# Attention, a dense layer and a routed mixture of experts on one core: who makes the low parts of the first weights, and how chunk 0 opens

## The chip, the cores and the metric

The kernel runs on one core of one Trainium2 chip. The metric is the device time of one execution in microseconds (us). Three runs of the kernel before gave 1522.58, 1522.92 and 1523.56 us, median 1522.92 us.

The engines by the names of the profile: PE (TensorE; PEld are its weight loads), DVE (VectorE), ACT (ScalarE), POOL (GpSimd) and SP (SyncE, which here only issues DMAs). Matrix products land in PSUM, in eight banks of 128 partitions by 512 float32 columns; everything else on the chip is SBUF.

## What is computed

```python
kv = np.einsum('bhsd,bhse->bhde', k, v)
out = np.einsum('bhsd,bhde->bhse', q, kv)
rms = np.sqrt(np.mean(out * out, axis=-1, keepdims=True) + 1e-06)
x = out / rms * g_norm                    # then heads side by side: 4608 tokens x 512
h = np.maximum(np.maximum(x @ w1, x @ w2), x @ w3)
x = h @ w_out                             # 512 -> 768 -> 512
logits = x @ w_gate + np.log1p(np.exp(x @ w_noise)) * noise
top2 = np.argpartition(-logits, 2, axis=1)[:, :2]
...
h = np.maximum(x[mask] @ w1[e], 0.0)      # 8 experts, 512 -> 1024 -> 512
out[mask] += top2_w[mask, k, None] * (h @ w2[e])
```

There are 8 batches of 576 tokens and 8 heads of 64.

## The kernel before

**Precision.** A float32 product is made of three faster ones. Each operand is split into a high part, which ACT rounds, and a low part, which is the operand less its high part; the passes are high x high, high x low and low x high (`g1_mm`: 12 matmuls of 512 or 256 columns for one group of 128 features).

**Tokens.** The 4608 tokens go in nine chunks of 512. A chunk is attended (`ao`, 64x64 products of Q with K-transposed-V), normalized, transposed (`xtrans_pe`) and split (`xtrans_hi` on ACT, `xtrans_lo` on DVE). The dense layer then takes 18 groups (`g1`), three for each 128 of the 768 hidden features, of which `g1_top` keeps the maximum in `HM` (the first of three by ACT, the others by DVE, both out of PSUM); `hsplit` splits it and `g2` multiplies by w_out. `route_a` and `route_b` pick the experts on DVE, and `scatter` writes rows to DRAM by indirect DMAs on POOL. Eight batches of 576 do not match nine chunks of 512, so chunk 1's first 256 tokens are done early, inside chunk 0 (the groups `eq`, which read the tiles `xA`, B_87 below).

**Chunk 0 and its weights.** The twelve weight slabs of the dense layer, W0 to W11 (W_70 to W_81 below; nine for w1 to w3, three for w_out), arrive as raw 64-bit halves and are made in chunk 0, one after another: `conv_lo` (ACT), `conv_hi` (two DVE instructions, lines 509 and 510), `conv_sq` (ACT), `conv_add` (DVE, line 518), `conv_top` (DVE, line 531), `conv_split` (ACT, line 535, the high part) and `conv_rest` (DVE, line 539, the low part). `conv_rest` reads two SBUF tiles and writes a third. A slab feeds two groups.

**The order in chunk 0** is set by a small planner (`task` and `run_tasks`): each task has an engine, a cost in us, the tasks it comes after, and an urgency; `run_tasks` appends the tasks to the engines' queues in the order in which they could start by these costs. At run time each engine takes its queue strictly in that order and waits where an input isn't there.

**K and V.** `kv_mm` makes K-transposed times V of a pair of heads from 576 rows: four steps of 128 rows and a last one of 64. For the last step the 64 rows stand in tiles whose other 64 partitions POOL has filled with zeros, so that all five steps have the same shape. For batch 0 the steps are the outer loop and the four pairs the inner one, each pair in a bank of its own; for the other batches `kv_pair` does a pair at a time, all four in one bank, which `kv_out` copies at once.

**The experts.** After chunk 8 the tokens are taken in units of 512, 256 or 128 rows of one expert (`unit`; `G1` and `G2` are its two products). The routing of chunk 8 and the table of units (`table`, a generator) run on DVE within the first units: `pump` says how many pieces of it go into which step. One step is one call of `G1` and what is due from `G2`.

```python
pump = {0: 1, 2: 1, 3: 2, 4: 2, 5: 2, 6: 2, 8: 1, 9: 1}
...
for _ in range(pump.get(step[0], 0)):
    next(tg, None)
```

Of the kernel before, what the change touches and what calls it, by code (L numbers as in the profile page):

```python
# [88 lines left out]
def body(tc, A, dbg=None):  # L89
# [61 lines left out]
    kvraw = {}  # L151

    def quarters(t):
        return [t[:, i * 512:(i + 1) * 512] for i in range(4)]

    def load_kv(b, part):
        if part == 0:
            SP.dma_start(KV0, A["kv4"][b, 0])
            kvraw[b] = [quarters(KV0)]
        elif part == 1:  # L160
            t = STG[b % 2]
            SP.dma_start(t, A["kv4"][b, 1])
            kvraw[b].append(quarters(t))
        else:
            t = STG[2]
            SP.dma_start(t[0:64, 0:1024], A["kvr"][b])
            kvraw[b].append((t[:, 0:512], t[:, 512:1024]))

    qbuf = [RB, KV0] + [RB] * 7

# [4 lines left out]
        SP.dma_start(qbuf[c][:, 0:2048], A["qT"][c])  # L175

    pad = st("pad", [128, XW])
    POOL.memset(HM[0][64:128, :], 0.0)
    POOL.memset(pad[64:128, 0:512], 0.0)
    POOL.memset(ones, 1.0)  # L180
    POOL.memset(RA[:, 2048:], 0.0)

# [2 lines left out]

    def kv_mm(b, p, s, out):
        r = kvraw[b]
        if s < 4:
            k, v = r[s // 2][2 * (s % 2):2 * (s % 2) + 2]
        else:  # L190
            k, v = r[2]
        for h in range(2):
            o = p * 128 + h * 64
            PE.matmul(out[HALF[h], :], k[:, o:o + 64], v[:, o:o + 64], start=s == 0, stop=s == 4)  # L194

    def kv_pair(b, p, bank):
        for s in range(5):
            kv_mm(b, p, s, bank[:, p * 64:(p + 1) * 64])

    def kv_out(b, bank):  # L200
        DVE.tensor_copy(KB[b % 2], bank[:, 0:256])

    ao_bank = {}

# [373 lines left out]
    load_w1(1)  # L578
    for f in (conv_lo, conv_hi, conv_sq, conv_add, conv_top, conv_split, conv_rest):
        f(0)  # L580
    for p in range(4):
        abank()
    for s in range(5):
# [5 lines left out]
    for p in range(4):  # L589
        (ACT.copy if p % 2 else DVE.tensor_copy)(KB[0][:, p * 64:(p + 1) * 64], AC[p][:, 0:64])  # L590

    zeroed = []

# [55 lines left out]
    def on_ring(name, n=1):  # L649
        return (name, n)  # L650
# [6 lines left out]
    for i in range(4):  # L657
        task(f"n0c{i}", "DVE", 0.65, ["n0b2"], lambda i=i: norm_c(0, i), 0)

        def t0(i=i):  # L660
            tr0[i] = xtrans_pe(0, i, None if i < 3 else abank())

        task(f"t0{i}", "PE", 0.44, [f"n0c{i | 1}"] + ([f"t0{i - 1}"] if i else []), t0, 0,
             on_ring(f"x0l{i}") if i < 3 else None)
# [3 lines left out]
    def kv1(p):  # L668
        if p == 0:
            bank_of["kv"] = hbank()  # L670
        kv_pair(1, p, bank_of["kv"])

    for p in range(4):
        task(f"kvp{p}", "PE", 0.6, ["kv1"] + [f"kvp{p - 1}" if p else "first0"], lambda p=p: kv1(p), 1,
             None if p else on_ring("kvo"))
    task("kvo", "DVE", 0.42, ["kvp3", "hi0"], lambda: kv_out(1, bank_of["kv"]), 0.3)
    task("q1", "SP", 2.6, ["kvp3", "w1"], lambda: load_q(1), 0)
    task("tri", "SP", 0.2, ["kvp3", "q1"], lambda: SP.dma_start(pad[:, 0:128], A["cst"][:, CST["tri"][0]:]), 9)

    for s in range(1, 12):  # L680
        if s > 1:
            task(f"w{s}", "SP", 2.6, [["kv1", "top0"], ["kvp3"], ["top1"]][s - 2] + [f"w{s - 1}"] if s < 5 else [f"top{s - 3}", f"w{s - 1}"], lambda s=s: load_w1(s), s)
        free_t = [f"add{s - 2}"] if s > 1 else []
        free_w = [f"rest{s - 2}"] if s > 1 else []
        if s == 11:
            free_w = free_w + ["gate_a0"]
        u = 2 + 0.1 * s if s > 1 else 0.4
        task(f"lo{s}", "ACT", 1.15, [f"w{s}"] + ["n0e"] * (s == 1), lambda s=s: conv_lo(s), u)
        task(f"op{s}", "DVE", 1.92, [f"w{s}"] + free_t + ["n0c3"] * (s == 1), lambda s=s: conv_hi(s), u)
        task(f"sq{s}", "ACT", 1.14, [f"op{s}"], lambda s=s: conv_sq(s), u - 1 if s > 1 else 0.05)  # L690
        task(f"add{s}", "DVE", 1.22, [f"op{s}", f"lo{s}"], lambda s=s: conv_add(s), u)
        task(f"top{s}", "DVE", 1.22, [f"add{s}", f"sq{s}"] + free_w, lambda s=s: conv_top(s), u)
        task(f"hi{s}", "ACT", 1.06, [f"top{s}"], lambda s=s: conv_split(s), u - 1)
        task(f"rest{s}", "DVE", 1.22, [f"hi{s}"], lambda s=s: conv_rest(s), u - 1)

    def passes(g, z):
        if g not in bank_of:
            bank_of[g] = abank() if g < 2 else hbank()
        for n in z:
            g1_mm(g, bank_of[g], n)  # L700
# [261 lines left out]
    for c in range(NCH):  # L962
        if c == NCH - 1:
            ctx1.close()
            sb2 = ctx.enter_context(tc.tile_pool(name="sb2", bufs=1, reuse_waits="tile"))
            xTu.append(xview(B2, sb2.tile([128, 2048], FR, name="xlo")))
        for g in range(18):
            misc1(c, g)
            if c > 0:
                g1(c, g)  # L970
        if c == 0:
            run_tasks({"PE": 16.8, "DVE": 19.0, "ACT": 18.2, "SP": 13.5},
                      {f"{n}0": (12.0, "DVE") for n in ("w", "lo", "op", "sq", "add", "top", "hi", "rest")})
        window(c)

# [300 lines left out]
def layout(q, k, v, g_norm, moe_w1, moe_w2, moe_w3, moe_w_out,  # L1276
# [34 lines left out]
```

## Time and profile before

| | |
|---|---|
| median of three runs | 1522.92 us (1522.58 to 1523.56) |
| the profiled execution, its own time | 1517.31 us |
| its span, first to last instruction | 1515.5 us |
| PE busy | 1489.0 us, 98% |
| PE's weight loads | 1279.2 us, 84% |
| DVE busy | 777.5 us, 51% |
| ACT busy | 658.6 us, 43% |
| POOL busy | 224.0 us, 15% |
| share of PE in the chain that ended last | 96% |

The profile comes from one execution; its time stands beside its span in the table, and the difference lies outside the span. Busy shares are of the span. The ends of matmuls are modelled, so that two neighbours can seem to overlap by some tenths of a us; a start-to-start distance is the safer reading. Chunk 0 fills the span up to about 118 us, chunks 1 to 8 the part up to about 680 us, and the experts the rest.

### The profile page before, as it was taken

The numbers are of one execution on the slowest core, as the hardware profiler recorded it, in microseconds if no ns is written. First come the engines' busy times: TensorE is split into PE (matmuls) and PEld (weight loads), VectorE is DVE, ScalarE is ACT, GpSimd is POOL, SyncE is SP. The second block draws the span as 40 slices with busy tenths as digits, with TensorE's granted clock in tenths as the row PEclk, the third lists the DMA queues.
The fourth block names the chain that finished last, engine by engine and source line by source line (L and its number), as shares of the span: only waits on it lengthen the run. The fifth ranks groups of instructions, "written<-read, shape, count | busy, mean of one in ns | idle before, by whom it ended". The sixth has DMA issues, their size and how long they took to land.

```text
span 1515.5 us, 23040 instructions
## 1 busy us (share of the span) xinstructions
PE 1489.0 (98%) x9268; PEld 1279.2 (84%) x9268; DVE 777.5 (51%) x1503; ACT 658.6 (43%) x1024; POOL 224.0 (15%) x331
## 2 busy tenths in 40 slices
PE   6999999999999999999999999999999999999997
PEld 5889989898989888898888888888888888888886
DVE  6985535454444445458444463544554544635443
ACT  4553424242424233343444454644654544536443
POOL 0000211112020202014111101201211111012012
PEclk9999999999999999999999999999999999999999
DMA  8322434142332303082777566745876665668444
GB/s 314 134 77 91 138 132 153 72 147 85 126 117 95 120 29 120 8 251 113 228 169 155 143 199 163 203 133 131 212 187 153 184 148 142 205 167 209 128 116 79
DMA packets 160340, 218.74 MB, mean 144 GB/s; under 512 B 125472, under 2 KB 125728, under 8 KB 143712
## 3 DMA queue, kind: packets, MB, share of 16 engines
q1 hardware_dynamic: 140272, 165.45, 35.3%
q0 software_dynamic: 19952, 51.73, 15.1%
q8 instruction: 74, 1.21, 0.3%
q14 instruction: 42, 0.34, 0.1%
HBM read 137.91 MB, written 51.72 MB: 125 GB/s over the span
## 4 chain that ended last, share of the span: by engine, by line
PE 96%; DVE 1%; DMA 1%; ACT 1%; issue 0%; POOL 0%; SPq 0%; POOLq 0%; DVEq 0%
PE bank L356 29%; PE bank L1185 27%; PE bank L1123 26%; PE bank L402 10%; PE bank L216 1%; PE bank L194 1%; PE bank L1137 1%; DMA RB<-qT 1%; PE bank L554 0%; DVE stat L237 0%; PE bank L546 0%; POOL out L1159 0%; PE bank L1148 0%; PE bank L275 0%; ACT B L279 0%
## 5 line engine op out<-in xcount | busy, mean ns | idle before, releaser
L356 PE MATMUL bank<-B,W 128*128 128x512 f32 (+1 forms) x2160 | 452.7, 369 | 2.3 <-DVE B L284 1.4
L356 PEld LDWEIGHTS bank<-B,W 128*128 128x128 f32 x2160 | 375.0, 188 | 70.6 <-ACT B L279 1.6
L1185 PE MATMUL bank<-W,B 128*128 128x512 f32 x1728 | 417.8, 390 | 0.0
L1185 PEld LDWEIGHTS bank<-W,B 128*128 128x128 f32 x1728 | 322.2, 188 | 65.3
L1123 PE MATMUL bank<-B,W 128*128 128x512 f32 (+1 forms) x1568 | 364.2, 370 | 0.0
L1123 PEld LDWEIGHTS bank<-B,W 128*128 128x128 f32 x1568 | 280.6, 188 | 52.4
L338 DVE TENSOR_TENSOR W<-G,W 128x1024 fp32r<-128x1024 f32 x184 | 222.6, 1224 | 116.5 <-ACT W L337 115.9
L1127 ACT ACTIVATE B<-bank 128x512 fp32r<-128x512 f32 (+1 forms) x160 | 88.7, 555 | 349.4 <-PE bank L1123 349.3
L1128 DVE SCALAR_TENSOR_TENSOR B<-bank,B 128x512 fp32r<-128x512 f32 (+1 forms) x160 | 101.9, 637 | 258.5 <-ACT B L1127 258.0
L337 ACT ACTIVATE W<-G 128x1024 fp32r<-128x1024 f32 x184 | 192.0, 1055 | 40.4 <-PE bank L1185 27.3
L402 PE MATMUL bank<-W,B 128*128 128x256 f32 (+1 forms) x1296 | 160.9, 284 | 0.3 <-DVE B L364 0.3
L402 PEld LDWEIGHTS bank<-W,B 128*128 128x128 f32 x1296 | 159.5, 188 | 1.4 <-DVE B L364 0.5
L475 POOL DMA_INDIRECT Xg<-RA,si x72 | 71.0, 986 | 516.6 <-issue 362.6
L374 DVE TENSOR_TENSOR hm<-hm,bank 128x512 f32<-128x512 f32 (+1 forms) x106 | 69.5, 656 | 115.0 <-PE bank L356 109.8
L360 ACT ACTIVATE B<-hm 128x512 fp32r<-128x512 f32 (+1 forms) x53 | 32.1, 606 | 183.1 <-DVE hm L374 183.1
L1159 POOL DMA_INDIRECT out<-xn,idt x37 | 60.5, 1635 | 264.4 <-ACT xn L1190 257.1
L1123 PE MATMUL bank<-xlo,W 128*128 128x512 f32 (+1 forms) x352 | 83.8, 360 | 0.0
L1123 PEld LDWEIGHTS bank<-xlo,W 128*128 128x128 f32 x352 | 61.3, 189 | 10.0
L1159 POOL DMA_INDIRECT out<-hm,idt x19 | 31.0, 1630 | 222.4 <-ACT hm L1190 219.4
L1159 POOL DMA_INDIRECT out<-x2T,idt x19 | 31.4, 1652 | 177.2 <-ACT x2T L1190 173.7
L372 ACT ACTIVATE hm<-bank 128x512 f32<-128x512 f32 (+1 forms) x53 | 30.3, 572 | 59.8 <-PE bank L356 49.2
L409 ACT COPY RA<-bank 128x256 uint16<-128x256 uint16 x72 | 25.7, 373 | 68.2 <-DVE RA L409 62.7
(196 smaller groups left out, 1047.9 us busy)
## 6 DMA issues: line engine op xcount, KB each, us to landing
G<-mw SPq DMA_DIRECT2D x92, 1024.0 KB, 5.0
G<-w1s SPq DMA_DIRECT2D x12, 1024.0 KB, 4.8
kv<-kv SPq DMA_DIRECT2D x8, 1024.0 KB, 7.2
G<-kv SPq DMA_DIRECT2D x8, 1024.0 KB, 10.7
RB<-qT SPq DMA_DIRECT2D x8, 1024.0 KB, 4.9
out<-pad POOLq DMA_DIRECT2D x5, 1280.0 KB, 5.7
out<-pad POOLq DMA_DIRECT2D x2, 1536.0 KB, 6.4
G<-kvr SPq DMA_DIRECT2D x6, 256.0 KB, 10.6
```

Of the source, the lines that this page charges most:

```text
L337: ACT.activation(w[:, 0:1024], src, AF.Copy)
L338: DVE.tensor_tensor(w[:, 1024:2048], src, w[:, 0:1024].bitcast(F), op=OP.subtract)
L356: PE.matmul(bank[:, 0:t1 - t0], w_in(g)[:, a, k, s], x[b][:, k, t0:t1], start=n == 0 and k == 0, stop=n == 2 and k == 3)
L360: ACT.activation(hTf(f)[:, 0, t0:t1], hm, AF.Copy)
L374: DVE.tensor_tensor(hm, hm, bank, op=OP.max)
L402: PE.matmul(x2b[i][z][:, 0:hi - lo], h[:, a, s], w[:, b, lo:hi], start=f == 0 and n == 0, stop=f == 5 and n == 2)
L475: i = POOL.indirect_dma_start(out=Xg, out_offset=bass.IndirectOffsetOnAxis(ap=idx, axis=0), in_=src, in_offset=None)
L1123: PE.matmul(bank[:, 0:n], w[:, a, k, s], x[b][:, k, 0:n], start=z == 0, stop=z == 11)
L1127: ACT.activation(h[:, 0, 0:n], bank[:, 0:n], AF.Relu)
L1128: DVE.scalar_tensor_tensor(h[:, 1, 0:n], bank[:, 0:n], 0.0, h[:, 0, 0:n].bitcast(F), op0=OP.max, op1=OP.subtract)
L1159: d = POOL.indirect_dma_start(out=A["out"], out_offset=bass.IndirectOffsetOnAxis(ap=idt[u % 3][:, i:i + 1], axis=0), in_=y, in_offset=None ...
L1185: PE.matmul(obank[i], h[:, a, s], w[:, b, ff % 2, :], start=ff == 0 and n == 0, stop=ff == 7 and n == 2)
```

## The change

Four things are changed. **(a)** The low part of each slab but the first is made by POOL, with the same instruction, and the planner gets a clock for POOL. **(b)** Chunk 0's first two groups are done in two halves of 256 tokens, each half with its three passes as soon as its tokens are split, in four banks instead of two; the fourth transpose takes a bank of the other ring. **(c)** The last 64 rows of K and V lie by heads, the pairs 0 and 1 in the lower 64 partitions and the pairs 2 and 3 in the upper; their products have 64 rows and no zeros; a batch's pairs come one after another, each with its four full steps in a bank of its own, then the last steps of the pairs in the order 0, 2, 1, 3; the copies out of the four banks are shared by DVE and ACT. POOL's three fills with zeros are gone, and one DMA takes the place of two. **(d)** The first pieces of the table go into other steps of the experts' first unit. The numbers of lines after line 178 shift: line 539 becomes 542, 356 becomes 359, 194 becomes 193, 374 becomes 377.

```diff
-            SP.dma_start(t[0:64, 0:1024], A["kvr"][b])
-            kvraw[b].append((t[:, 0:512], t[:, 512:1024]))
+            SP.dma_start(t[:, 0:512], A["kvr"][b])
+            kvraw[b].append(t[:, 0:512])
...
-    POOL.memset(HM[0][64:128, :], 0.0)
-    POOL.memset(pad[64:128, 0:512], 0.0)
...
-        if s < 4:
-            k, v = r[s // 2][2 * (s % 2):2 * (s % 2) + 2]
-        else:
-            k, v = r[2]
         for h in range(2):
-            o = p * 128 + h * 64
+            if s < 4:
+                k, v = r[s // 2][2 * (s % 2):2 * (s % 2) + 2]
+                o = p * 128 + h * 64
+            else:
+                k, v = r[2][HALF[p // 2], 0:256], r[2][HALF[p // 2], 256:512]
+                o = p % 2 * 128 + h * 64
             PE.matmul(out[HALF[h], :], k[:, o:o + 64], v[:, o:o + 64], start=s == 0, stop=s == 4)
...
+    def kv_all(b, banks):
+        for p in range(4):
+            for s in range(4):
+                kv_mm(b, p, s, banks[p][:, 0:64])
+        for p in (0, 2, 1, 3):
+            kv_mm(b, p, 4, banks[p][:, 0:64])
+
+    def kv_outs(b, banks):
+        for p in range(4):
+            (ACT.copy if p % 2 else DVE.tensor_copy)(KB[b % 2][:, p * 64:(p + 1) * 64], banks[p][:, 0:64])
...
-        DVE.tensor_tensor(lo, t, hi.bitcast(F), op=OP.subtract)
+        (POOL if s else DVE).tensor_tensor(lo, t, hi.bitcast(F), op=OP.subtract)
...
-    for s in range(5):
-        for p in range(4):
-            kv_mm(0, p, s, AC[p][:, 0:64])
+    first = [abank() for p in range(4)]
+    kv_all(0, first)
...
-            tr0[i] = xtrans_pe(0, i, None if i < 3 else abank())
+            tr0[i] = xtrans_pe(0, i)
...
+    task("kvp3", "PE", 2.3, ["kv1", "first100"], kv1, 1, on_ring("kvo", 4))
...
-        task(f"rest{s}", "DVE", 1.22, [f"hi{s}"], lambda s=s: conv_rest(s), u - 1)
+        task(f"rest{s}", "POOL", 2.3, [f"hi{s}"], lambda s=s: conv_rest(s), u - 1)
+
+    def half_pass(g, x, n):
+        if not half_of:
+            half_of.update({(a, b): abank() for a in range(2) for b in range(2)})
+        g1_mm(g, half_of[g, x], n, xT, x * 256, x * 256 + 256)
+
+    def half_top(g):
+        for x in range(2):
+            g1_top(g, half_of[g, x][:, 0:256], HM[0][:, x * 256:x * 256 + 256])
...
-    for z in range(3):
-        task(f"first{z}", "PE", 1.82, [["x0h3", "hi0", "n0c2"], ["x0l3", "first0"], ["rest0", "first1"]][z],
-             lambda z=z: (passes(0, [z]), passes(1, [z])), 2)
+    for g in range(2):
+        for x in range(2):
+            for z in range(3):
+                task(f"first{g}{x}{z}", "PE", 0.48,
+                     [[f"x0h{2 * x + 1}", "hi0"], [f"x0l{2 * x + 1}"], ["rest0"]][z] + [f"first{g}{x}{z - 1}"] * (z > 0),
+                     lambda g=g, x=x, z=z: half_pass(g, x, z), 2 + 0.1 * g)
...
-            POOL.memset(STG[2][64:128, 0:1024], 0.0)
...
-            bank = abank()
-            for p in range(4):
-                kv_pair(c + 1, p, bank)
-            kv_out(c + 1, bank)
+            banks = [abank() for p in range(4)]
+            kv_all(c + 1, banks)
+            kv_outs(c + 1, banks)
...
-            run_tasks({"PE": 16.8, "DVE": 19.0, "ACT": 18.2, "SP": 13.5},
+            run_tasks({"PE": 16.8, "DVE": 19.0, "ACT": 18.2, "SP": 13.5, "POOL": 10.0},
...
-    pump = {0: 1, 2: 1, 3: 2, 4: 2, 5: 2, 6: 2, 8: 1, 9: 1}
+    pump = {0: 1, 3: 2, 4: 2, 5: 2, 6: 3, 8: 1, 9: 1}
...
-    a["kvr"] = kv[:, 512:].reshape(NB, 64, 1024)
+    a["kvr"] = kv[:, 512:].reshape(NB, 64, 2, 2, 256).transpose(0, 3, 1, 2, 4).reshape(NB, 128, 512)
```

What this does to the engines' queues, at three places. **PE, batch 0's K and V**, the first products of the program (kv_92 holds the first two steps' rows, G_84 the next two's, hm_96 the last 64; bank_109 to bank_112 are the pairs' banks). Before, rows 5 to 12 of the queue, which follow four that are the same as the first four here:

```order
L194 MATMUL bank_109<-kv_92 64x64 x2
L194 MATMUL bank_110<-kv_92 64x64 x2
L194 MATMUL bank_111<-kv_92 64x64 x2
L194 MATMUL bank_112<-kv_92 64x64 x2
L194 MATMUL bank_109<-G_84 64x64 x2
L194 MATMUL bank_110<-G_84 64x64 x2
L194 MATMUL bank_111<-G_84 64x64 x2
L194 MATMUL bank_112<-G_84 64x64 x2
```

Now, rows 1 to 12:

```order
L193 MATMUL bank_109<-kv_92 64x64 x4
L193 MATMUL bank_109<-G_84 64x64 x4
L193 MATMUL bank_110<-kv_92 64x64 x4
L193 MATMUL bank_110<-G_84 64x64 x4
L193 MATMUL bank_111<-kv_92 64x64 x4
L193 MATMUL bank_111<-G_84 64x64 x4
L193 MATMUL bank_112<-kv_92 64x64 x4
L193 MATMUL bank_112<-G_84 64x64 x4
L193 MATMUL bank_109<-hm_96 64x64 x2
L193 MATMUL bank_111<-hm_96 64x64 x2
L193 MATMUL bank_110<-hm_96 64x64 x2
L193 MATMUL bank_112<-hm_96 64x64 x2
```

All sixteen products with kv_92 stood ahead of the first that needs G_84; now four of them do.

**PE, the groups of the weight slabs 3 to 5** (W_73 to W_75; a row of 512 columns that reads B_85 is chunk 0's, a row of 256 that reads B_87 is one of chunk 1's early groups, whose weights are older). Before:

```order
L356 MATMUL bank_106<-B_85,W_73 128x512 x8
L356 MATMUL bank_107<-B_87,W_71 128x256 x12
L356 MATMUL bank_106<-B_85,W_73 128x512 x4
L356 MATMUL bank_108<-B_85,W_73 128x512 x12
L356 MATMUL bank_105<-B_85,W_74 128x512 x8
L356 MATMUL bank_106<-B_87,W_72 128x256 x12
L356 MATMUL bank_105<-B_85,W_74 128x512 x4
L356 MATMUL bank_107<-B_85,W_74 128x512 x12
L356 MATMUL bank_108<-B_85,W_75 128x512 x8
L356 MATMUL bank_105<-B_87,W_72 128x256 x12
L356 MATMUL bank_108<-B_85,W_75 128x512 x4
L356 MATMUL bank_106<-B_85,W_75 128x512 x12
```

Now, up to slab 6:

```order
L359 MATMUL bank_107<-B_85,W_73 128x512 x8
L359 MATMUL bank_108<-B_87,W_70 128x256 x12
L359 MATMUL bank_107<-B_85,W_73 128x512 x4
L359 MATMUL bank_105<-B_85,W_73 128x512 x12
L359 MATMUL bank_106<-B_87,W_70 128x256 x12
L359 MATMUL bank_107<-B_85,W_74 128x512 x12
L359 MATMUL bank_108<-B_85,W_74 128x512 x12
L359 MATMUL bank_105<-B_85,W_75 128x512 x12
L359 MATMUL bank_106<-B_85,W_75 128x512 x12
L359 MATMUL bank_107<-B_85,W_76 128x512 x12
L359 MATMUL bank_108<-B_85,W_76 128x512 x12
L359 MATMUL bank_105<-B_87,W_71 128x256 x12
```

From slab 3's first row to slab 8's last there were six early groups in PE's queue, and there are three now; ahead of slab 3 there were three and there are none. The other fifteen stand between and behind the transposes of the last three slabs (line 549, `gate_a`).

**DVE, two slabs in the middle of chunk 0.** Before:

```order
L539 TENSOR_TENSOR W_73<-RA,W_73 128x1024
L518 ISA G_83<-G_83,RB 128x1024x2
L531 SCALAR_TENSOR_TENSOR RA<-G_83 128x1024
L509 TENSOR_SCALAR RB<-G_82 128x1024
L510 SCALAR_TENSOR_TENSOR RB<-G_82,RB 128x1024
L374 TENSOR_TENSOR hm_96<-hm_96,bank_108 128x512
L539 TENSOR_TENSOR W_74<-RA,W_74 128x1024
L518 ISA G_82<-G_82,RB 128x1024x2
L374 TENSOR_TENSOR xn_93<-xn_93,bank_106 128x256
L531 SCALAR_TENSOR_TENSOR RA<-G_82 128x1024
```

Now:

```order
L521 ISA G_83<-G_83,RB 128x1024x2
L534 SCALAR_TENSOR_TENSOR RA<-G_83 128x1024
L512 TENSOR_SCALAR RB<-G_82 128x1024
L513 SCALAR_TENSOR_TENSOR RB<-G_82,RB 128x1024
L377 TENSOR_TENSOR hm_96<-hm_96,bank_105 128x512
L377 TENSOR_TENSOR xn_93<-xn_93,bank_106 128x256
L521 ISA G_82<-G_82,RB 128x1024x2
L534 SCALAR_TENSOR_TENSOR RA<-G_82 128x1024
```

The low parts (line 539) are gone from DVE; eleven rows of line 542 stand in POOL's queue, one behind another, ahead of what POOL does for chunk 0's routing.

## Rows read from the trace of the kernel before

**Rows 1.** Busy time by stretches: us, then each engine's busy us, granted clock, DMA share, GB/s.

```profile
49.20:95.00 45.80, 45.79 (x249) 39.62 (x250) 43.23 (x50) 25.24 (x29) 0.00 (x0) 1.00 0.41 139
```

**Rows 2.** PE's waits: line, what for, us in total, times, longest.

```profile
PE bank L356 <- DVE B L284: 1.4, 1, 1.4
...
PE bank L356 <- ACT B L279: 0.9, 1, 0.9
PE bank L460 <- DVE Cb L448: 0.8, 1, 0.8
...
PE bank L546 <- DVE RA L531: 0.5, 1, 0.5
```

**Rows 3.** Timeline, 8 to 18 us: start, us, what [idle before <-releaser].

```profile
8.11 1.98 PE L194 MATMUL bank<-kv 128*64 128x64 f32 x32 [8.11 <-DMA kv<-kv]
...
11.02 1.97 PE L194 MATMUL bank<-G 128*64 128x64 f32 x32 [0.93 <-DMA G<-kv]
...
12.78 1.07 PE L194 MATMUL bank<-pad,hm 128*64 128x64 f32 x16
...
14.53 3.11 PE L216 MATMUL bank<-kvt,RB 64*64 64x64 f32 x128 [0.68 <-DMA RB<-qT]
```

**Rows 4.** Timeline, 23 to 28 us, the opening of chunk 0.

```profile
23.05 2.46 ACT L279 ACTIVATE B<-bank,gn 128x512 fp32r<-128x512 f32 x4 [1.66 <-PE bank L275]
...
24.27 0.38 PE L275 MATMUL bank<-cst,x2T 128*128 128x128 f32 x2
...
25.57 2.11 PE L356 MATMUL bank<-B,W 128*128 128x512 f32 x8 [0.92 <-ACT B L279]
```

**Rows 5.** The chain that ended last, 105 to 115 us: start, us, what.

```profile
108.20 2.96 PE bank L356 x24
```

**Rows 6.** The same chain, 180 to 440 us.

```profile
185.81 27.21 PE bank L356 x120
...
427.73 2.48 PE bank L194 x80
...
435.88 2.02 PE bank L216 x128
```

**Rows 7.** DVE's groups, 49.2 to 95 us: busy us, mean ns, idle before.

```profile
L531 DVE SCALAR_TENSOR_TENSOR RA<-G 128x1024 f32<-128x1024 f32 x7 | 8.6, 1223 | 0.2
...
L539 DVE TENSOR_TENSOR W<-RA,W 128x1024 fp32r<-128x1024 f32 x6 | 7.3, 1219 | 0.0
L509 DVE TENSOR_SCALAR RB<-G 128x1024 int32<-128x1024 int32 x7 | 4.8, 687 | 0.0
```

**Rows 8.** PE's groups, 10 to 120 us: busy us, mean ns, idle before.

```profile
L554 PE MATMUL bank<-wgn,G 128*128 128x16 f32 x48 | 5.6, 259 | 0.0
...
L546 PE MATMUL bank<-cst,RA 128*128 128x128 f32 x24 | 3.2, 276 | 0.5 <-DVE RA L531 0.5
```

**Rows 9.** Timeline of POOL, 100 to 104 us.

```profile
100.69 0.95 POOL L895 MEMSET G<- 64x1024 f32 x1 [98.55 <-PE bank L554]
101.71 0.85 POOL L595 CAST trib<-pad 128x128 bf16<-128x128 f32 x1
...
102.65 0.52 POOL L597 MEMSET pad<- 128x520 f32 x1
```

**Rows 10.** Timeline of DVE, the same stretch.

```profile
101.20 1.22 DVE L531 SCALAR_TENSOR_TENSOR RA<-G 128x1024 f32<-128x1024 f32 x1
...
102.67 1.06 DVE L509 TENSOR_SCALAR RB<-G 128x1024 int32<-128x1024 int32 x1
```

**Rows 11.** Timeline of DVE, 234 to 237.5 us.

```profile
235.47 0.67 DVE L300 COPY kv<-xn 128x512 uint16<-128x512 uint16 x1
...
236.76 0.43 DVE L300 COPY kv<-x2T 128x512 uint16<-128x512 uint16 x1
```

**Rows 12.** Timeline of POOL, 234 to 237 us.

```profile
234.94 0.97 POOL L475 DMA_INDIRECT Xg<-RA,si  x1 [0.22 <-DVE B L364]
235.91 0.26 POOL L473 MEMSET spacer<- 1x1 f32 x1
```

More of the change, by code (lines that the diff above doesn't have):

```diff
@@ L187, in kv_mm @@
         r = kvraw[b]
-        if s < 4:
-            k, v = r[s // 2][2 * (s % 2):2 * (s % 2) + 2]
-        else:
-            k, v = r[2]
         for h in range(2):
-            o = p * 128 + h * 64
-            PE.matmul(out[HALF[h], :], k[:, o:o + 64], v[:, o:o + 64], start=s == 0, stop=s == 4)
-    def kv_pair(b, p, bank):
-        for s in range(5):
-            kv_mm(b, p, s, bank[:, p * 64:(p + 1) * 64])
-    def kv_out(b, bank):
-        DVE.tensor_copy(KB[b % 2], bank[:, 0:256])
+            if s < 4:
[4 more added lines that the diff above has]
+                o = p % 2 * 128 + h * 64
+            PE.matmul(out[HALF[h], :], k[:, o:o + 64], v[:, o:o + 64], start=s == 0, stop=s == 4)
+    def kv_all(b, banks):
[7 more added lines that the diff above has]
+            (ACT.copy if p % 2 else DVE.tensor_copy)(KB[b % 2][:, p * 64:(p + 1) * 64], banks[p][:, 0:64])
     ao_bank = {}
@@ L564, in load_kv_first @@
         SP.dma_start(STG[2], A["kv4"][b, 1])
-        SP.dma_start(HM[0][0:64, :], A["kvr"][b][:, 0:512])
-        SP.dma_start(pad[0:64, 0:512], A["kvr"][b][:, 512:1024])
-        kvraw[b] = [quarters(KV0), quarters(STG[2]), (HM[0], pad[:, 0:512])]
+        SP.dma_start(HM[0], A["kvr"][b])
+        kvraw[b] = [quarters(KV0), quarters(STG[2]), HM[0]]
     def warm(n):
@@ L580, in body @@
         f(0)
-    for p in range(4):
-        abank()
-    for s in range(5):
-        for p in range(4):
-            kv_mm(0, p, s, AC[p][:, 0:64])
+    first = [abank() for p in range(4)]
+    kv_all(0, first)
     load_kv_first(1)
     SP.dma_start(wgn, A["wgn"])
-    for p in range(4):
-        (ACT.copy if p % 2 else DVE.tensor_copy)(KB[0][:, p * 64:(p + 1) * 64], AC[p][:, 0:64])
+    kv_outs(0, first)
     zeroed = []
@@ L660, in t0, with kv1 @@
         def t0(i=i):
-            tr0[i] = xtrans_pe(0, i, None if i < 3 else abank())
+            tr0[i] = xtrans_pe(0, i)
         task(f"t0{i}", "PE", 0.44, [f"n0c{i | 1}"] + ([f"t0{i - 1}"] if i else []), t0, 0,
-             on_ring(f"x0l{i}") if i < 3 else None)
+             on_ring(f"x0l{i}"))
         task(f"x0h{i}", "ACT", 0.69, [f"t0{i}"], lambda i=i: xtrans_hi(i, tr0[i]), 0.1)
         task(f"x0l{i}", "DVE", 0.69, [f"x0h{i}"], lambda i=i: xtrans_lo(i, tr0[i]), 0.3)
[L668 to L676, printed above, removed]
+    def kv1():
+        bank_of["kv"] = [hbank() for p in range(4)]
+        kv_all(1, bank_of["kv"])
+    task("kvp3", "PE", 2.3, ["kv1", "first100"], kv1, 1, on_ring("kvo", 4))
+    task("kvo", "DVE", 0.45, ["kvp3", "hi0"], lambda: kv_outs(1, bank_of["kv"]), 0.3)
     task("q1", "SP", 2.6, ["kvp3", "w1"], lambda: load_q(1), 0)
@@ L693, in body @@
         task(f"hi{s}", "ACT", 1.06, [f"top{s}"], lambda s=s: conv_split(s), u - 1)
-        task(f"rest{s}", "DVE", 1.22, [f"hi{s}"], lambda s=s: conv_rest(s), u - 1)
+        task(f"rest{s}", "POOL", 2.3, [f"hi{s}"], lambda s=s: conv_rest(s), u - 1)
+    half_of = {}
+    def half_pass(g, x, n):
[5 more added lines that the diff above has]
+            g1_top(g, half_of[g, x][:, 0:256], HM[0][:, x * 256:x * 256 + 256])
     def passes(g, z):
         if g not in bank_of:
-            bank_of[g] = abank() if g < 2 else hbank()
+            bank_of[g] = hbank()
         for n in z:
@@ L703, in hm0 @@
         return X2f if g // 3 == 4 else HM[0]
-    for z in range(3):
-        task(f"first{z}", "PE", 1.82, [["x0h3", "hi0", "n0c2"], ["x0l3", "first0"], ["rest0", "first1"]][z],
-             lambda z=z: (passes(0, [z]), passes(1, [z])), 2)
+    for g in range(2):
[4 more added lines that the diff above has]
+                     lambda g=g, x=x, z=z: half_pass(g, x, z), 2 + 0.1 * g)
+    last_of = [[f"first{g}{x}2" for x in range(2)] for g in range(2)]
+    done = last_of[0] + last_of[1]
     for g in range(18):
         if g > 1:
-            task(f"gp{g}", "PE", 1.82, ["x0l3", f"hi{g // 2}", "first2"] + ([f"gq{g - 1}"] if g > 2 else []),
+            task(f"gp{g}", "PE", 1.82, ["x0l3", f"hi{g // 2}"] + done + ([f"gq{g - 1}"] if g > 2 else []),
                  lambda g=g: passes(g, [0, 1]), 2, on_ring(f"ev{g}"))
@@ L716, in body @@
         task(f"ev{g}", "DVE" if g % 3 else "ACT", 0.69 if g % 3 else 0.58,
-             [f"gq{g}" if g > 1 else "first2", "kvp3"] + ([f"ev{g - 1}"] if g else []) + hm_free,
-             lambda g=g: g1_top(g, bank_of[g], hm0(g)), 0.5)
+             ([f"gq{g}"] if g > 1 else last_of[g]) + ["kvp3"] + ([f"ev{g - 1}"] if g else []) + hm_free,
+             lambda g=g: g1_top(g, bank_of[g], hm0(g)) if g > 1 else half_top(g), 0.5)
     last = [f"eq{e}" for e in range(18)]
@@ L726, in body @@
         if i == 0:
-            task("ao0", "PE", 1.0, ["q1", "kvo", "x0l3"], lambda: ao(1, 0, [abank(), abank()]), 0)
+            task("ao0", "PE", 1.0, ["q1", "kvo", "x0l3", "ev0"] + done, lambda: ao(1, 0, [abank(), abank()]), 0)
         task(f"n1s{i}", "ACT", 0.6, ["ao0", "t03"], lambda i=i: norm_sq(1, i, x1[i]), 0.6)
@@ L919, in misc1 @@
         if 0 < c < NB - 1 and g == 10:
-            bank = abank()
-            for p in range(4):
-                kv_pair(c + 1, p, bank)
-            kv_out(c + 1, bank)
+            banks = [abank() for p in range(4)]
+            kv_all(c + 1, banks)
+            kv_outs(c + 1, banks)
         if 0 < c < NCH - 1 and g >= 12:
```

## The prediction

> **What bounds the kernel now.** I read the busy time by stretches first, to see where PE is not full. From 50 us on it always is, in chunk 0 too: 45.79 of 45.80 us between 49.2 and 95 [rows 1]. So time is lost at the start, at the few waits that are listed for PE [rows 2], and at the end. The same row says what is nearly full beside PE: DVE works 43.23 of these 45.8 us, and POOL 0.00. The waits of PE that the change aims at are small: 0.9 us for ACT at the opening of chunk 0, 1.4 us for line 284, 0.5 us for line 531, 0.8 us for the table's first piece at line 460. Together that is 3.6 us, so a gain can't be much over that; a loss can, where the work on the weights comes to set PE's pace. The timelines of the first 28 us [rows 3, 4] show the opening, the chain that ended last the price of a matmul at full flow [rows 5, 6], and DVE's groups the price of a slab [rows 7].
>
> The sum is made against the profiled execution, 1517.31 us, which was 5.61 us quicker than the median of the three runs; I add the difference that comes out to the median, 1522.92 us. About 0.2%, 3.0 us, is what a measurement of this kernel can tell from no change.
>
> **The change, part by part.**
>
> *K and V of batch 0.* Before, 32 records that need only the first tile ran in the 2 us in which the second was under way [rows 3]. Now eight of them come first; the other 24 and the 32 of the second tile start at 11.02 us. At the 62 ns of these rows (1.98 us by 32) they take 3.5 us, to 14.5 us. The last 16 records took 1.07 us with 128 rows; with 64 rows their shape is that of `ao`, 3.11 us by 128, 24 ns, so 0.4 us in all. Then a copy, and `ao` begins at about 15.2 us instead of 14.53: **+0.7 us** (from +0.4, if the copies are fully beside it, to +1.4, if the last rows cost what they did). All of the opening waits behind `ao`, so this is on the path. Batch 1's tiles are asked for some 4 us later, since the first tile is read to the end later; its products come at 28 us, which covers that. One DMA issue and three fills go; nothing waits for them.
>
> *Halves of tokens.* PE is done with the transposes at 24.65 us and waited until 25.57 us for the last high part, four of which took 2.46 us from 23.05 on [rows 4]. The first half needs two of the four, which are there at 24.3 us: −0.9 us. But 48 matmuls of 256 columns replace 24 of 512: 2.96 us by 24 is 0.123 us each [rows 5], 27.21 by 120 is 0.227 [rows 6], so 5.9 us for 5.4, +0.5 us. Net **−0.4 us**. The two more evictions are on ACT and DVE beside PE.
>
> *The last rows, batches 1 to 7.* 80 records took 2.48 us, 31 ns each; those of 64 rows take 2.02 us by 128, 16 ns [rows 6]. If the 16 last ones come to that: 16 × 15 ns × 7 = **−1.7 us** (0 if the bank per pair brings nothing, and 0.1 us worse per batch at most if the change of shape drains the array). The four copies take no longer than the one did, spread over two engines that have room.
>
> *The routing.* The wait of 0.8 us goes [rows 2], as the product stands a step of at least 2.7 us later. By step 6 the same ten pieces are through, so nothing behind it moves: **−0.8 us** (0 to −0.8).
>
> *Low parts on POOL, if nothing disturbs DVE.* The waits of 1.4 and 0.5 us lose their cause. In their place PE asks for slab 3 right behind chunk 1's transposes, and its high part stands on ACT behind the two copies of these transposes, about 1.3 us that used to be covered by early groups; and the low part of slab 2 comes 0.6 us after PE wants it, as POOL is slower. So **0 us** (−1.9 if both new waits fail to come, +2 if POOL is half as slow again). Without a disturbance the sum is +0.7 − 0.4 − 1.7 − 0.8 + 0 = **−2.2 us**.
>
> *Low parts on POOL, with DVE kept out.* No row has a subtraction on POOL, but several show POOL and DVE getting in each other's way. DVE's line 509, 0.69 us as a rule [rows 7], took 1.06 us when it met POOL's fill, which ended 0.4 us later [rows 9, 10]. DVE's copy took 0.67 us instead of 0.43 when it began inside one of POOL's DMA issues, and POOL's fill of one element, begun inside that copy, lasted until the copy ended [rows 11, 12]. And POOL's cast of 128 columns took 0.85 us: it began inside DVE's line 531, which reads two SBUF tiles, and ended 0.15 us after that instruction's end [rows 9, 10]. Each time the later one stood until the earlier was through. The subtraction reads two SBUF tiles, and of DVE's work on a slab lines 510, 518 and 531 do so too, and line 509 is the form that was held.
> The Trainium skill's page "SBUF — State Buffer", section "Who interferes with whom", says that GpSimd's ports are VectorE's second pair, and that of a VectorE instruction with two SBUF inputs and a GpSimd instruction that reads SBUF the second fully blocks until the first is done; the cast agrees, a held DVE instruction of two inputs is in no row here. By the rows that show a held DVE instruction alone, only line 509 would be held, 0.69 us of each slab, and the sum would stay near −2 us; by the rule, all four are.
>
> What that costs: in the new order PE asks for slabs 3 to 8 with three early groups between them, so 12 groups at 12 × 0.227 and three at 12 × 0.123 us: 37.1 us, 6.2 us a slab. DVE without the low parts needs (43.23 − 7.3) / 6.5 = 5.5 us a slab (six of line 539 and seven of the others lie in that stretch) [rows 1, 7]. So DVE keeps up with 0.7 us in hand, unless POOL keeps it out. How long: a fill of 1024 columns took 0.95 us with nothing to read [rows 9]; the cast's 0.15 us beyond its wait is 1.2 us for 1024 columns of one operand, 2.4 for two; with its wait, 0.85 × 8 = 6.8. I take 2.2 us, nearest to two passes of the fill and to the cast without its wait. Some 0.4 us of that is beside evictions, which read one operand from PSUM. Then a slab takes 5.5 + 2.2 − 0.4 = 7.3 us, 1.1 over PE's pace, × 6 = 6.6 us. For slabs 9 to 11 PE has five early groups (7.4 us) and the gates' products ((5.6 + 3.2) / 3 a slab [rows 8]), 5.4 us a slab, against 0.69 + 3 × 1.22 + 0.4 + 2.2 = 6.9 on DVE: 1.5 × 3 = 4.5 us. On slabs 1 and 2 POOL itself waits for DVE about half of 1.2 us, twice: 1.2 us. **+12.3 us** in all, on PE's path, since the early groups that once filled such waits now stand behind the last slab. At 0.95 us it would be +1, at 2.8 us +17.
> The skill's page "GPSIMD Engine Reference", section 3.1, gives 4497 ns for such an instruction of 2048 columns; half of it is an estimate of 2.25 us, by which the sum would be 0.5 us more.
>
> Behind POOL's eleven subtractions stand only chunk 0's fills and scatters; the first scatter came at 150 us, which covers them.
>
> **Forecast**: −2.2 + 12.3 = +10.1 us, 1533.0 us, slower.
>
> **The rivals.**
>
> *DVE isn't held by POOL's reads* (or line 509 alone is): −2.2 us, 1520.7 us, no change that can be told. For it: no row has a held DVE instruction with two SBUF inputs, and the cast's 0.85 us could be the price of a first call. Against it: the cast's end at 0.15 us behind line 531, and three other pairs that all stood in line. 30%.
>
> *Faster.* DVE isn't held, and the two waits aren't replaced: −2.2 − 1.9 = −4.1 us, 1518.8 us. It ends on the other side of the forecast. The place is PE behind chunk 1's transposes; it decides whether ACT has slab 3's high part by then. For it: DVE, freed of 7.3 us in that stretch, may finish slab 3 early. Against it: ACT's order, in which two copies and the high part stand in a row. 15%.
>
> *The change does less than it says*: the last rows don't overlap, so −1.7 falls to 0. That shifts each case by 1.7 us and turns none around.
>
> **How the numbers follow.** The forecast has 55%: POOL's time and how much DVE can do beside it make it from +4 (about 1.4 us) to +17, its own range 1527 to 1540 us. The undisturbed cases have 45%, from −4.1 to +2. The range of 8 in 10 goes from 1519.4 to 1540: it leaves out most of the faster case and the far end of POOL's price. Slower by over 0.2%: 0.55; within: 0.30; faster: 0.15.
>
> **What would show it.** Right: in the stretch from 50 to 110 us DVE's lines 513, 521 and 534 with mean times well over 1.23 us; POOL's line 542 near 2.2 us or longer; PE waiting several times for POOL or ACT at line 359 and for DVE at line 549, 10 us or more together; chunk 0 ending near 128 us. Wrong: DVE's means as before and PE without waits after 50 us; then the rival holds. `ao` later than 16 us or a batch's K and V still at 2.48 us would make the small terms wrong.

## The result, and the profile after

The change takes 1537.6 us (median of six, 1536.88 to 1538.68) where the kernel before, run beside it, takes 1523.11 (1522.2 to 1524.27): a ratio of 1.0095, 95% interval 1.0084 to 1.0105, so **14.5 us slower** (12.8 to 16.0). The forecast was slower, 1533.0 us, range 1519.4 to 1540.

Busy time by stretches, of the change (the columns of [rows 1]):

```profile
49.20:95.00 45.80, 39.73 (x180) 30.91 (x180) 44.94 (x41) 24.82 (x27) 15.49 (x6) 1.00 0.42 138
95.00:110.00 15.00, 11.61 (x86) 11.38 (x87) 13.93 (x13) 8.04 (x11) 5.25 (x2) 0.89 0.00 1
```

PE, which was busy for 45.79 us of the first stretch [rows 1], lacks 6.1 us of it, and does 180 matmuls in place of 249. DVE has lost six low parts, and is busier than before: 44.94 us instead of 43.23. PE's waits from 30 to 130 us, of the change:

```profile
PE bank L359 <- POOL W L542: 3.7, 7, 0.9
PE bank L359 <- ACT W L538: 3.5, 3, 1.8
PE bank L549 <- DVE RA L534: 2.0, 1, 2.0
PE bank L359 <- DVE xn L377: 1.5, 1, 1.5
```

They come to 10.7 us (a fifth row has 0.3 us), where the same stretch of the kernel before had 1.9 us for lines 284 and 531 [rows 2] and 0.3 us for line 364. DVE's groups of the change, 49.2 to 95 us:

```profile
L513 DVE SCALAR_TENSOR_TENSOR RB<-G,RB 128x1024 int32<-128x1024 int32 x7 | 15.1, 2163 | 0.2
L521 DVE CUSTOM_DVE_ANT_0 G<-G,RB 128x2048 uint16<-128x2048 uint16 x6 | 9.9, 1643 | 0.1
L534 DVE SCALAR_TENSOR_TENSOR RA<-G 128x1024 f32<-128x1024 f32 x6 | 7.3, 1225 | 0.7
L512 DVE TENSOR_SCALAR RB<-G 128x1024 int32<-128x1024 int32 x7 | 4.8, 687 | 0.0
L377 DVE TENSOR_TENSOR hm<-hm,bank 128x512 f32<-128x512 f32 x6 | 4.1, 680 | 0.0
L367 DVE TENSOR_TENSOR B<-hm,B 128x512 fp32r<-128x512 f32 x3 | 3.7, 1223 | 0.0
```

Undisturbed, line 513 takes 1.23 us, 521 1.22 and 367 0.69. So the excess is 7 × 0.93 + 6 × 0.42 + 3 × 0.53 = 10.7 us for the six subtractions of this stretch, 1.8 us each. Line 377, which reads PSUM, has no excess. Where the excess comes from stands in the two timelines, 58 to 70 us, first DVE's:

```profile
58.83 1.22 DVE L513 SCALAR_TENSOR_TENSOR RB<-G,RB 128x1024 int32<-128x1024 int32 x1
59.97 0.68 DVE L377 TENSOR_TENSOR hm<-hm,bank 128x512 f32<-128x512 f32 x1
60.57 0.41 DVE L377 TENSOR_TENSOR xn<-xn,bank 128x256 f32<-128x256 f32 x1
60.90 2.49 DVE L521 CUSTOM_DVE_ANT_0 G<-G,RB 128x2048 uint16<-128x2048 uint16 x1
...
65.99 3.42 DVE L513 SCALAR_TENSOR_TENSOR RB<-G,RB 128x1024 int32<-128x1024 int32 x1
```

and POOL's:

```profile
59.36 2.94 POOL L542 TENSOR_TENSOR W<-RA,W 128x1024 fp32r<-128x1024 f32 x1 [6.21 <-ACT W L538]
65.93 2.40 POOL L542 TENSOR_TENSOR W<-RA,W 128x1024 fp32r<-128x1024 f32 x1 [3.63 <-ACT W L538]
```

The subtraction takes 2.40 us by itself. At 59.36 us it began inside line 513, and took 0.54 us longer: it waited. Inside it, both rows of line 377 ran at their usual time. Line 521 began inside it, and ended 1.09 us behind its end (63.39 against 62.30); line 513, begun 0.06 us after the second subtraction, ended 1.08 us behind that (69.41 against 68.33). Each held instruction did nearly all its work after POOL was through.

### The profile page after: what moved, and what is told of

Read it like the earlier page. It is cut to its first block, busy times and chain, and to the rows that moved or that the text cites. A ratio compares the mean times of both kernels' runs of the same rounds, so it can differ in the third digit from the quotient of the medians.

```text
span 1535.1 us, 23110 instructions
## 1 busy us (share of the span) xinstructions
PE 1496.2 (97%) x9292; PEld 1282.0 (84%) x9292; DVE 784.3 (51%) x1500; ACT 661.6 (43%) x1039; POOL 249.7 (16%) x339
## 4 chain that ended last, share of the span: by engine, by line
PE 54%; issue 0%; POOL 0%; ACT 0%; POOLq 0%
PE bank L1194 27%; PE bank L1132 26%; PE bank L1146 1%; PE bank L405 0%; POOL out L1168 0%; PE bank L1157 0%; ACT W L340 0%; ACT x2T L1199 0%; POOLq L1269 0%; ACT RA L412 0%; PE bank L1088 0%; POOL spacer L1167 0%; PE bank L463 0%; PE bank L464 0%
```

## The experiments

In the table the place is where PE begins chunk 1's second half of attention (line 216, 219 in the change), a product that stands behind all of the dense layer's groups, the early ones too, in every one of these queues (where a * stands, 12 products with w_out, some 1.4 us by their starts, stand ahead of it as well; they win nothing, as PE there waits 1.7 us for line 364, 367 in the change, behind the place, and 0.2 to 0.3 us in the other runs). Each place is that of one profiled execution; ratios are to the kernel before, beside each run.

| run | place, us | ratio (95%) |
|---|---|---|
| the kernel before; once more, unchanged | 116.85; 116.41 | 1; 1.0003 (0.9994 to 1.0012) |
| the change | 129.75 | 1.0095 (1.0084 to 1.0105) |
| low parts back on DVE | 119.84* | 1.0001 (0.9992 to 1.0010) |
| POOL's low parts alone | 126.96 | 1.0096 (1.0081 to 1.0112) |
| the change's order, on DVE | 123.00 | 1.0035 (1.0023 to 1.0047) |
| fills on POOL | 116.12 | 0.9983 (0.9973 to 0.9993) |
| copies on POOL | 116.55 | not comparable |
| DVE's order, on POOL | 127.15* | 1.0073 (1.0058 to 1.0089) |
| halves alone | 119.24* | 1.0011 (1.0001 to 1.0020) |
| last rows and routing | 115.94 | 0.9959 (0.9946 to 0.9973) |
| the same again | 115.90 | 0.9969 (0.9957 to 0.9980) |
| routing alone | 115.89 | 0.9989 (0.9980 to 0.9999) |
| DVE, slab 2 first | 115.62 | 0.9970 (0.9958 to 0.9983) |

**Which part is it?** The change without (a), and (a) without the rest:

```diff
-        (POOL if s else DVE).tensor_tensor(lo, t, hi.bitcast(F), op=OP.subtract)
+        DVE.tensor_tensor(lo, t, hi.bitcast(F), op=OP.subtract)
-        task(f"rest{s}", "POOL", 2.3, [f"hi{s}"], lambda s=s: conv_rest(s), u - 1)
+        task(f"rest{s}", "DVE", 1.22, [f"hi{s}"], lambda s=s: conv_rest(s), u - 1)
```

> The change with the low parts back on DVE, in the planner too: what is left is the halves, K and V's last rows and the routing. If POOL's subtractions are the cause (my theory), the loss goes: 1520 to 1523 us, DVE's lines 513 and 521 back at 1.23 us each, chunk 0's dense layer ending near 117 us instead of 129.75. If the halves or the four banks are the cause (first rival), 1530 us or more stays.

> The kernel before with only the low parts moved to POOL, and its planner told 2.3 us for them. Theory: the whole loss is here, +12 to +16 us, 1535 to 1539 us, with DVE's lines 510 and 518 at 3.4 and 2.5 us wherever they begin inside a POOL subtraction. Rival (halves or banks): within 3 us of the kernel before, 1520 to 1526 us.

1.0001 and 1.0096: by the ratios the whole loss is (a), and the halves are not its cause. By the places (a) alone makes 10.1 of the change's 12.9 us; what the other 2.8 are is not separated. In the first run DVE's lines 513 and 521 are back at means of 1226 and 1221 ns; in the second DVE's lines 510 and 518 have means of 1.54 and 2.69 us in 49.2 to 95 us. The first run's place is nonetheless 3 us late: the 1.4 us of w_out, one wait of PE of 2.1 us for slab 2's high part, and a stretch of 3.4 us at clock 0.5 (1.2 of 2.4 GHz) right behind it. That profiled execution (1519.88 us) is the slowest of its eleven, whose median is 1518.02 where the kernel before beside it had 1517.2.

**Is it the order or the holding?** The change's queues, with DVE as the one that subtracts (the first line of the diff above alone):

> The change with PE's, ACT's and SP's queues as they are in it, but DVE does the subtraction, at the place in the program where the planner put POOL's. Theory (DVE is held by POOL): DVE works 5.5 + 1.2 = 6.7 us a slab where PE asks for one in 6.2, some 0.5 us on each of six slabs and about as much on the last three, +3 to +5 us over the kernel before: 1525 to 1528 us. Rival (the new order of PE with its early groups late is the cause, whoever subtracts): 1534 to 1538 us.

1.0035, +5.3 us: the theory's size. And the reverse, the queues planned for DVE with POOL as the one that subtracts (the second line of that diff alone):

> The queues of the run with the low parts back on DVE (the planner is told DVE, 1.22 us), but POOL does the subtractions. DVE is held as in the change; PE has its early groups between the slabs to fill the waits. Theory (DVE's pace sets when the last slab is there, and the new order of PE adds to it, as it leaves 15 early groups behind or among the last slabs): the last line 534 ends near 109 us again, PE's waits are fewer, and some half of the loss stays, +5 to +9 us over the kernel before. Rival (a toll on each slab that no order of PE's hides): +12 to +15 us as in the change.

1.0073 against 1.0001 with the same queues on DVE: +11 us. The places give less, 7.3 us (127.15 against 119.84): the two runs are from different chips, and behind chunk 0 the one on POOL has gaps of PE that nothing in the profile ends, and the other none. The largest row of them, 135 us on:

```profile
PE bank L1194 <- issue: 3.2, 4, 1.6
```

Over the kernel before the place is 10.3 us later, between the two expectations. So early groups between the slabs hide little. PE's rows show why: it waited 4.6 us in two waits for line 538, and the last line 534 ended at 120.0 us instead of the change's 108.9, since DVE has to take the early groups' maxima between the slabs as well. The part of the theory that gave the late early groups half of the loss falls. By the places, POOL in DVE's stead costs 7.3 us in this order and 6.8 in the change's (129.75 against 123.00); the order itself costs 2.6 with POOL (129.75 against 127.15) and 3.2 with DVE (123.00 against 119.84), of 12.9 us in all. Against the fills below, which leave DVE neither the work nor more than a little hindrance, POOL's subtractions cost 13.6.

**Reading or writing?** POOL's subtraction replaced by two fills of the same tile, and by a copy:

```diff
-        (POOL if s else DVE).tensor_tensor(lo, t, hi.bitcast(F), op=OP.subtract)
+        POOL.tensor_copy(lo[:, 0:1], hi[:, 0:1].bitcast(F))
+        for _ in range(2):
+            POOL.memset(lo.bitcast(F), 0.0)
```

> The change with two fills of the low part's tile on POOL in place of each subtraction, behind a copy of one column that waits for the high part as the subtraction did; so POOL writes as much or more in about 2 us and reads next to nothing. It leaves out the low parts of slabs 1 to 11. Theory (POOL's reads of SBUF hold DVE): DVE's lines 513 and 521 stay at 1.23 us, at most line 512 is held as in the row where it met a fill; 1520 to 1525 us. Rival (any work of POOL on these tiles holds DVE, reads or not): lines 513 and 521 at 2 us and more on the mean, 1531 us or more.

DVE's groups beside the fills, 49.2 to 95 us:

```profile
L513 DVE SCALAR_TENSOR_TENSOR RB<-G,RB 128x1024 int32<-128x1024 int32 x8 | 9.8, 1226 | 0.3
...
L521 DVE CUSTOM_DVE_ANT_0 G<-G,RB 128x2048 uint16<-128x2048 uint16 x8 | 9.8, 1221 | 0.1
L512 DVE TENSOR_SCALAR RB<-G 128x1024 int32<-128x1024 int32 x8 | 6.3, 786 | 0.0
```

POOL's, 30 to 115 us:

```profile
L547 POOL MEMSET W<- 128x1024 f32 x22 | 21.9, 996 | 1.3
```

POOL works 2.0 us a slab, nearly as long as the subtraction, and lines 513 and 521 don't notice. Line 512, with one SBUF input, does: 786 ns in the mean instead of 687, and 1.48 us where it began inside a fill. The time is near the forecast's undisturbed sum, −2.6 us where −2.2 was worked out.

```diff
+        POOL.tensor_copy(lo, hi.bitcast(F))
```

> The change with a copy of the high part on POOL in place of each subtraction: one SBUF tile read and one written. It leaves out the low parts of slabs 1 to 11, which become copies of the high parts. Theory, first form (any POOL instruction that reads SBUF keeps out a DVE instruction with two SBUF inputs): DVE's lines 513 and 521 are held until the copy's end, with means well over 1.23 us; with a copy of 1.2 to 2.3 us the time is 2 to 14 us over the fills', 1517 to 1529 us where the kernel before has 1517. Rival (two reads on POOL are needed): lines 513 and 521 stay at 1.23 us as beside the fills, and the time is the fills', 0.9983 of the kernel before.

The wrong low parts send tokens to other experts, so that only chunk 0 of this run compares with the others. One row of DVE, and POOL's beside it:

```profile
67.39 2.04 DVE L513 SCALAR_TENSOR_TENSOR RB<-G,RB 128x1024 int32<-128x1024 int32 x1
```

```profile
67.32 1.04 POOL L545 CAST W<-W 128x1024 fp32r<-128x1024 f32 x1 [4.17 <-ACT W L538]
```

Line 513 ended 1.07 us behind the copy's end: one operand read on POOL is enough to hold it. The means from 49.2 to 95 us are 1416 ns for line 513 and 1308 for 521, less than "well over" 1.23 us: few rows of either were held. A copy that isn't held itself takes 1.04 us, not 2.40, and the place is 116.55 us, no later than before. What costs is the length of POOL's reading, and the expectation's lower end (2 us over the fills) was still too dear: 0.4 us.

**The small parts.** The halves on the kernel before:

```diff
+        g1_mm(g, half_of[g, x], n, xT, x * 256, x * 256 + 256)
```

> The kernel before with only the first two groups in halves of tokens. By the prediction's term -0.4 us, no difference that can be measured: 0.998 to 1.002 of the kernel before, the first dense matmul near 24.4 us instead of 25.57 and the 48 of 256 columns 0.5 to 0.9 us longer than the 24 of 512. Rival (the four banks and the moved transposes cost more than they give): 1.002 or more, with a new wait of PE before 50 us.

1.0011: within the expectation, and its rival's mark is there too. The first dense matmul came at 25.45 us, not near 24.4, as `ao` began at 15.12 us in this execution. Two rows of PE's waits, 30 to 120 us:

```profile
PE bank L356 <- ACT W L535: 2.1, 1, 2.1
PE bank L546 <- DVE RA L531: 0.5, 1, 0.5
```

The new wait is for slab 2: the planner has put its line 531 behind a sum of squares, which DVE waited 1.05 us for. Told that this step is urgent, it puts it first (on top of the low parts on DVE):

```diff
-        task(f"top{s}", "DVE", 1.22, [f"add{s}", f"sq{s}"] + free_w, lambda s=s: conv_top(s), u)
+        task(f"top{s}", "DVE", 1.22, [f"add{s}", f"sq{s}"] + free_w, lambda s=s: conv_top(s), 0.3 if s == 2 else u)
```

> The change with the low parts on DVE, and the planner told that line 534 of slab 2 is urgent, so that it stands ahead of the first group's copy and the sums of squares in DVE's queue (it ended at 41.2 us in the run with the low parts on DVE, at 37.3 us where the queue had it first). Theory: the 2.1 us that PE waited there for slab 2's high part go, the early groups stand between the slabs as in the kernel before, and all of halves, rows and routing is left: -1.5 to -2.5 us, 0.9984 to 0.9990 of the kernel before, with chunk 0's attention of chunk 1 near 116 us instead of 119.84. Rival (another slab is late in its place): 1.000 or more.

The 2.1 us wait is gone, and the place is 115.62 us: 2.8 us better than with slab 2 late, the 1.4 us of w_out set aside, and 4.2 better behind the next wait, for line 367 (123.57 against 127.79). At 0.9970, −4.6 us, this version **beats both kernels**, by more than the 1.5 to 2.5 us that were expected. By the starts of the same products in both traces, 2.1 us of it are gaps and half clock that the kernel before, run again below, has and this one hasn't; that the edit is what removes those is not shown.

Last rows and routing on the kernel before, twice, and the routing alone:

```diff
+    pump = {0: 1, 3: 2, 4: 2, 5: 2, 6: 3, 8: 1, 9: 1}
```

> The kernel before with only K and V's last rows by heads and the routing a step later. By the trace of the change: a batch's K and V 2.41 us instead of 2.48, times seven, -0.5 us, and the wait of 0.8 us at line 460 gone: -1.3 us, 0.9991 of the kernel before (0.9985 to 1.000). By the prediction's own term (-1.7 - 0.8 + 0.7) it would be -1.8 us. Rival (chunk 0's order, which shifts with the four banks of batch 1, gives it back): 1.000 or more, with a new wait before 120 us.

> The same kernel as in the run with K and V's last rows and the routing alone, which came out at 0.9959 where its terms (0.5 + 0.8 us) give 0.9991. If the terms are all there is, it comes to 0.998 to 1.000 now; the rest was PE's gaps put down to issue, which the profiles show between 150 and 170 us and near 580 us in some executions (1.5 + 1.1 us in that profile, none in the profile of the kernel before) and which differ from chip to chip. If the smaller products or the four banks themselves give 6 us, it stays at 0.995 to 0.997.

> The kernel before with only the pieces of the table in other steps. The wait of 0.8 us at line 460 goes and none comes in its place: -0.8 us, 0.9995 of the kernel before, not to be told from no change. Rival (the pieces wait elsewhere): the wait appears at another line after 680 us.

−6.2, −4.7 and −1.7 us. The routing's interval takes in its 0.8 us; the other two are well over their 1.3, and the guess that the surplus would be gone the second time was wrong.

> The kernel before, unchanged, against itself, to see in its profile what its executions of 1522 to 1526 us spend over the profiled one of 1517.31 us, which had no gap of PE put down to issue. Theory (those gaps and the half clock behind them are the difference): where it takes 1522 us or more, the profile shows some 3 to 6 us of issue gaps from 150 us on and a stretch at clock 0.5, and the ratio is 1.000 within 0.1%; where it takes 1517 us, none. Rival: the extra time lies elsewhere, in DMA waits or outside the span.

PE's waits from 140 us on, of the kernel before, run again (its profiled span is 1522.0 us):

```profile
PE bank L194 <- issue: 1.5, 4, 0.4
PE bank L216 <- issue: 1.0, 1, 1.0
PE bank L1185 <- issue: 1.0, 2, 0.6
PE bank L460 <- DVE Cb L448: 0.8, 1, 0.8
```

and of the last rows and routing, again (1516.4 us):

```profile
PE bank L193 <- issue: 1.6, 4, 0.4
PE bank L219 <- issue: 0.9, 2, 0.5
```

The stretch from 155 to 160 us, first of the kernel before:

```profile
155.00:160.00 5.00, 4.64 (x43) 4.39 (x44) 0.92 (x3) 0.00 (x0) 0.12 (x2) 0.66 0.14 54
```

then of the last rows and routing:

```profile
155.00:160.00 5.00, 4.77 (x112) 4.49 (x115) 1.54 (x6) 1.10 (x5) 0.00 (x0) 1.00 0.14 53
```

The theory holds: the execution of 1523.85 us has 3.5 us of gaps that wait for nothing the profile shows, and a stretch at half clock, 155.5 to 158.9 us, as the first four end; the one of 1517.31 us had neither. By the starts of the same products this makes 6.5 us, which would explain why the profiled execution stood 5.61 us under the median. In these runs it goes with the chip: on one, 23 executions of the kernel before took 1516.30 to 1518.61 us, and the profiles of the four runs made there have no such gap; on two others they took 1521.59 to 1526.36 us, and each profile taken there has some. Both kernels have the gaps near 153 us and 580 us. The gaps at 722 us and the half clock, 1.2 and 0.85 us by the starts of the same products in both traces, are in one only; with 1.1 for routing, 0.8 between 161 and 684 us (the smaller K and V products are 0.4 of them), 0.5 up to 116 us and 0.5 at 153 us they make the 4.9 us by which the two traces differ at PE's last product (the spans differ by 5.6). Why that kernel is spared, and what PE waits for there, is open.

## Why the prediction was right, point by point

**Holding, +12.3 us.** Right in mechanism and size. The step "2.2 less 0.4 beside evictions" gave 1.8 us a slab, and 1.8 was measured; POOL's time was 2.40 us rather than 2.2. Against the fills, the same queues with lines 513 and 521 not held, the place is 13.6 us later, 1.65 of them the half clock below. Two numbers of the working were a little off and changed nothing: POOL's fill ended 0.50 us after line 509 began, not 0.4 [rows 9, 10], and at 2.8 us a subtraction the steps add up to nearly +18, not +17. It answers to the Trainium skill's page "SBUF — State Buffer", section "Who interferes with whom", in three ways that the traces bear out: a DVE instruction with two SBUF inputs is kept out by a POOL instruction that reads SBUF (3.42 us for line 513), not by one that only writes (1.23 beside the fills), and DVE's `tensor_scalar`, which the page lists as able to use both port pairs, also by one that writes (1.48 us for line 512). The estimate of 2.25 us for the subtraction from the Trainium skill's page "GPSIMD Engine Reference", section 3.1, was 6% short of the 2.40 us of the row.

**One detail of it was wrong**: line 534 was to be held as well. It never was (1225 ns): POOL's subtraction starts when ACT has the high part, which is behind that slab's line 534, so that it meets lines 512, 513 and 521 of the next slab and line 367 (line 512 once, 2.88 us at 99.80 us).

**The sum left out the clock.** Behind the 2.01 us wait PE's granted clock was 0.5 (1.2 of 2.4 GHz) for 3.4 us. PE's timeline of the change:

```profile
96.84 1.09 PE L549 MATMUL bank<-cst,RA 128*128 128x128 f32 x8 [2.01 <-DVE RA L534]
97.69 4.61 PE L359 MATMUL bank<-B,W 128*128 128x256 f32 x24
```

The 24 products took 4.61 us where 24 such take 2.96 at full clock [rows 5]: 1.65 us more. Not every such wait was followed by it: behind one of 2.03 us, at 99.72 us of the change's order on DVE, the clock stayed at 1.00.

**K and V of batch 0, +0.7 us.** Wrong, by 0.65: `ao` began at 14.58 us, not 15.2. The change's rows of PE:

```profile
10.60 0.69 PE L193 MATMUL bank<-G 128*64 128x64 f32 x8 [1.75 <-DMA G<-kv]
...
13.78 0.71 PE L193 MATMUL bank<-hm 64*64 64x64 f32 x16
14.58 2.94 PE L219 MATMUL bank<-kvt,RB 64*64 64x64 f32 x128
```

The 56 records behind the second tile took 3.2 us where 3.5 had been taken, and began 0.4 us earlier, as the tile came earlier; the last sixteen and the copy took 0.8 us where 0.7 had been.

**The last rows, −1.7 us.** Mis-sized: a batch takes 2.41 us instead of 2.48, −0.5 us in seven. The timeline of batch 1 in the change:

```profile
30.07 0.40 PE L193 MATMUL bank<-G 128*64 128x64 f32 x8
30.40 0.46 PE L193 MATMUL bank<-hm 64*64 64x64 f32 x16
30.79 0.39 PE L359 MATMUL bank<-B,W 128*128 128x256 f32 x1
```

Sixteen records take 0.39 us, 24 ns each, as the first batch's had been costed, not the 16 of a long row of `ao`; and the first of them starts 0.10 us later than the pace of 29 ns of the records before gives. That is the loss "if the change of shape drains the array", which I had kept as an end and not in the value.

**Halves, −0.4 us, and routing, −0.8 us.** The opening of chunk 0 in the change:

```profile
24.48 3.98 PE L359 MATMUL bank<-B,W 128*128 128x256 f32 x28
28.39 0.45 PE L193 MATMUL bank<-kv 128*64 128x64 f32 x8
```

The first dense product began at 24.48 us, where the forecast's −0.9 us had put it at 24.65; 28 of the halves' products fill the 3.9 us to 28.39, 0.139 each where 0.123 was taken. At that price (an estimate for the other 20) 48 of them cost 1.2 us more than the 24, and nothing is left of the 0.4 us. Line 463 is no longer among PE's waits, and the routing is worth 1.1 us rather than 0.8 by the traces above. What the step on the halves missed is not in the change at all: with DVE's low parts the planner's order around slab 2 costs more than the halves give.

**No disturbance, −2.2 us.** The fills' −2.6 us show a total that was right, in part by luck, for a case that did not come: between the traces of the kernel before and of the fills, both without gaps of PE, 0.7 us are won up to the place, where the terms add up to nothing, 0.9 from there to the experts, where 1.5 had been taken, and 1.1 by the routing. Nor do these and the 13.6 us make the measured 14.5: −2.6 + 13.6 is 11.0. The change's own trace has 4.6 us of gaps behind chunk 0, the kernel before run again 3.5, and between these two PE's last products are 13.5 us apart, with 13.3 at the place. So what the smaller parts win behind the place is lost there again, in part to gaps that no run explains.

## What to carry to other kernels

Before work goes from DVE to POOL, look at which of DVE's instructions stand beside it: those that read two SBUF tiles stop for as long as POOL reads. Here 1.22 us of DVE's own time were replaced by 1.8 us of DVE held, on an engine that was 94% busy; by these numbers it could pay only with a POOL instruction clearly shorter than the DVE instruction that it replaces, and no run has one that did: the copy of 1.04 us cost little, but left the low parts out. A planner that books POOL's time on POOL alone will then order the other engines for a pace that DVE can't keep.

## What the runs showed of the hardware that was not expected

POOL's read of a single tile is enough to hold DVE (2.04 us for line 513 beside a copy of 1.04 us), and a fill on POOL nearly as long as a subtraction (two of 1.0 us) leaves the two-input forms alone. PE stood for 3.5 us in gaps that no engine or DMA of the profile ends, in an execution of one and the same kernel that took 1523.85 us, and not in one of 1517.31 us: a difference between two kernels of that size needs traces of both from the same chip, or it is put down to the wrong edit.
